# Half blocks and memory terms of an attention kernel: one product of 128 rows for both heads in place of two products of 64 rows

## The chip, the core and the metric

The kernel runs on one core of a Trainium2 chip. The metric is the time of one execution on the device in microseconds (us). Engines are named as in the profile: PE (TensorE, the matrix engine), PEld (its weight loads), DVE (VectorE), ACT (ScalarE), POOL (GpSimd), SP (SyncE, which issues the transfers here).

## The reference, cut to what matters

```python
# q, k, v: (B=2, H=8, S=576, D=64); M_prev (B,H,D,D); z_prev (B,H,D); beta (H)
a = softmax(causal(q @ k.T / 8));  local = a @ v
q_p = elu(q) + 1
mem_out = (q_p @ M_prev) / (q_p @ z_prev + 1e-6)
x = g * mem_out + (1 - g) * local                  # g = sigmoid(beta), per head
x = elu(x @ w_in) @ w_out                          # 1152 x 512, d_ff 2048
out = sum_e p[:, e] * (relu(x @ w1[e]) @ w2[e])    # 4 experts, 1024 wide
```

## The kernel before, in words

Two heads are worked on at once: head 0 of a pair lies on partitions 0 to 63, head 1 on 64 to 127. Twelve units do the attention. The four F units (`F0` to `F3`, one for each pair of heads) take the first 192 rows of both batches; eight R units (`R00`, `R10`, `R01`, ...: batch and pair) take the other 384 rows of a batch. Each unit makes scores (`score`, tiles `sF`, `sR`), exponentials (`ptF`, `ptR`), transposes them with an identity (`transposes`, tiles `tF`, `tR`), copies the transposes to SBUF (`evac`, tiles `pfF`, `pfR`) and multiplies them with values (`values`). `mem` multiplies the feature map of the queries (`ppF`, `ppR`) with the memory. Values and memory are held in one tile `rv` (`rvF`, `rvR`) of entries of 65 columns: 64 columns and one that gives the denominator. `sum_a`, `sum_i`, `sum_f`, `mem_a`, `mem_i`, `mem_f`, `both` and `turn` divide, add and transpose back into `x`.

A tile of 128 queries has full blocks of 128 keys for each head (`odd` 0 or 1 in the list `BLOCKS`), and one half block (`odd` 2): 64 keys of head 0 on partitions 0 to 63, 64 keys of head 1 on partitions 64 to 127. An R unit has three tiles with 4, 3 and 2 full blocks for each head: 18 full blocks and 3 half blocks, in groups of four (`trans`, `evac`, `values` of a group). The half block of a tile comes last, and takes two products of 64 rows (line 1384), one for each head. `mem` takes two products of 64 rows for each tile (line 1244). All results go to one tile `sums` of two PSUM banks, one for each head; a bank holds memory terms in its first half and values in its second.

The products of attention here are of plain float32: the profile shows each as two weight loads and two matmuls ("records"). The dense layers use a float32 in two rounded parts: three matmuls for one product (lines 278 to 280, `mm3`).

The order of the work is made by a planner (`Plan.order`) while the program is written: each step has an engine, an assumed cost, a rank and the steps that it needs, and the planner starts on each engine the step of lowest rank that can start. Where it thinks that PE would wait, in the first 140 us, it puts matmuls of zeros there (`keep_busy`, `nothing`, line 304). Dense work of the rows of the F units (`ua`, `da`, then `ub`, `db`) fills PE between the steps of the R units. Weights of the first dense layer come as 64-bit words: lines 225, 231 and 235 (ACT, DVE, DVE) make float32 of them, lines 245 and 249 (ACT, POOL) split them into `wh` and `wl`. When the last R unit is done, DVE, ACT and POOL make sums of its blocks (`xT1` to `xT4`, lines 702 to 718, and of weights `s`, line 601) for the second stage (`pa10A`, ...).

Of the kernel before, what the change touches and what calls it, by code (L numbers as in the profile page):

```python
# [8 lines left out]
F32 = mybir.dt.float32  # L9
# [7 lines left out]
B, H, S, D = 2, 8, 576, 64  # L17
# [3 lines left out]
P = 128  # L21
NPART = 4
DV = D + 1
# [7 lines left out]
TILES = {"F": [(64, 192), (64, 192), (0, 64)], "R": [(448, 576), (320, 448), (192, 320)]}  # L31
# [6 lines left out]
HALVES = {"F": 4, "R": 8}  # L38
MEMORY = {"F": 8, "R": 11}
ENTRIES = {"F": 10, "R": 12}  # L40

BLOCKS = {
    kind: [
        b for t, (_, ext) in enumerate(tiles)
        for b in [(t, odd, j) for odd in (0, 1) for j in range(ext // P)] + [(t, 2, ext // P)]
    ]
# [13 lines left out]
def tile_kernel(  # L60
# [12 lines left out]
    nc = tc.nc  # L73
# [97 lines left out]
    FEWEST = {"F": 1, "R": 0}  # L171
# [863 lines left out]

    def values_cost(blocks):

        return sum(0.224 if odd < 2 else 0.45 for _, odd, _ in blocks)

# [98 lines left out]
    def plan_unit(plan, kind, b, c, start, spare, slack):  # L1138
# [4 lines left out]
        width = sum(ext for _, ext in tiles)  # L1143
        widest, entries = 1344, ENTRIES["R"]
# [21 lines left out]
        def load_v():  # L1166
            unit["rv"] = atile([P, entries, DV], F32, tag="rv", name=f"rv{uid}")[:, :ENTRIES[kind]]
            nc.sync.dma_start(out=unit["rv"], in_=vm[kind][c] if kind == "F" else vm[kind][b, c])
# [64 lines left out]
        def side(what):  # L1233
            keep_busy(at["sums"][:, 0, 256 * what:256 * what + 256], 2 * FEWEST[kind])
            return at["sums"][:, :, 256 * what:256 * what + nt * DV].rearrange("p a (t d) -> p a t d", d=DV)

        def mem():
            unit["om"] = side(0)
# [129 lines left out]
        def values(g):  # L1368
            if g == 0:
                unit["ov"] = side(1)  # L1370
            for n, (t, odd, j) in enumerate(groups[g]):
                col, pf, nb = P * n, unit["p", g], tiles[t][1] // P
                if odd < 2:
                    at_ = t * 2 + odd if kind == "F" else odd * full + (nb - 1 - j if odd else j)
                    nc.tensor.matmul(  # L1375
                        unit["ov"][:, odd, t], pf[:, col:col + P], unit["rv"][:, at_], start=j == 0, stop=False
                    )
                    continue
                for bi, r0, r in parts_of(t):

                    at_ = HALVES[kind] + (t + bi if len(parts_of(t)) > 1 else t)
                    for o in (0, 1):
                        rows = slice(D * o, D * o + D)
                        nc.tensor.matmul(  # L1384
                            unit["ov"][r0:r0 + r, o, t], pf[rows, col + r0:col + r0 + r], unit["rv"][rows, at_],
                            start=nb == 0, stop=True,
                        )

        for g, blks in enumerate(groups):
# [12 lines left out]
            add(  # L1402
                f"values{g}", "pe", values_cost(blks), lambda g=g: values(g),
                [f"evac{g}", "load_v"] + [f"values{g - 1}"] * (g > 0), ["ov"] * (g == 0), ["ph"] + ["rv", "nm", "nm"] * final,
# [177 lines left out]
```

## Time and profile before

| what | value |
|---|---|
| time, median of 3 runs | 728.83 us (728.65 to 729.18) |
| the profiled execution: its own time | 729.03 us |
| its span in the trace | 727.2 us (1.83 us lie around it) |
| PE busy | 717.5 us, 99% of the span |
| POOL, DVE, ACT busy | 425.7, 396.7, 354.2 us |

The busy time of PE includes matmuls of zeros and matmuls at half clock, and matmuls overlap in the pipeline; so the starts of successive rows say more than the durations.

### The profile page before, as it was taken

The numbers are of one execution on the slowest core, as the hardware profiler recorded it, in microseconds if no ns is written. First come the engines' busy times: TensorE is split into PE (matmuls) and PEld (weight loads), VectorE is DVE, ScalarE is ACT, GpSimd is POOL, SyncE is SP. The second block draws the span as 40 slices with busy tenths as digits, with TensorE's granted clock in tenths as the row PEclk, the third lists the DMA queues.
The fourth block names the chain that finished last, engine by engine and source line by source line (L and its number), as shares of the span: only waits on it lengthen the run. The fifth ranks groups of instructions, "written<-read, shape, count | busy, mean of one in ns | idle before, by whom it ended". The sixth has DMA issues, their size and how long they took to land.

```text
span 727.2 us, 11034 instructions
## 1 busy us (share of the span) xinstructions
PE 717.5 (99%) x4255; PEld 643.9 (89%) x4255; DVE 396.7 (55%) x846; ACT 354.2 (49%) x610; POOL 425.7 (59%) x256
## 2 busy tenths in 40 slices
PE   9989999999999999998999999999999999999997
PEld 5768998888889888897999999998998989899896
DVE  4887785434353443435537474873635546364562
ACT  7768877454444543444568373753323324243130
POOL 5468688665536442259878763597656456664210
PEclk9999999999999999999999999999999999999999
DMA  7677985434233041221423021112312203021002
GB/s 260 214 267 266 388 294 165 143 106 136 87 108 109 31 138 32 85 91 55 159 88 116 30 87 59 59 33 84 116 40 77 88 29 117 30 88 58 1 1 87
DMA packets 23541, 80.36 MB, mean 110 GB/s; under 512 B 2881, under 2 KB 2881, under 8 KB 23489
## 3 DMA queue, kind: packets, MB, share of 16 engines
q1 hardware_dynamic: 23488, 79.66, 32.6%
q8 instruction: 33, 0.54, 0.3%
q14 instruction: 20, 0.16, 0.1%
HBM read 68.90 MB, written 10.75 MB: 110 GB/s over the span
## 4 chain that ended last, share of the span: by engine, by line
PE 96%; POOL 2%; DVE 1%; issue 0%; ACT 0%
PE db L278 9%; PE db L280 9%; PE db L279 9%; PE sums L1375 5%; PE da L278 5%; PE da L279 5%; PE da L280 5%; PE ub L278 3%; PE sR L1297 3%; PE ub L280 3%; PE ub L279 3%; PE tR L1359 3%; PE sums L1384 2%; PE ua L278 2%; PE ua L280 2%; PE ua L279 2%
## 5 line engine op out<-in xcount | busy, mean ns | idle before, releaser
L249 POOL TENSOR_TENSOR wl<-wr,wh 128x1024 fp32r<-128x1024 f32 x72 | 171.9, 2391 | 178.7 <-ACT wh L245 140.0
L245 ACT ACTIVATE wh<-wr 128x1024 fp32r<-128x1024 f32 x72 | 75.7, 1056 | 96.5 <-PE db L279 55.8
L278 PE MATMUL db<-wh,hb 128*128 128x512 f32 x288 | 115.6, 401 | 0.0
L280 PE MATMUL db<-wl,hb 128*128 128x512 f32 x288 | 113.4, 394 | 2.2 <-POOL wl L249 2.2
L279 PE MATMUL db<-wh,hb 128*128 128x512 f32 x288 | 113.0, 392 | 0.0
L997 DVE SCALAR_TENSOR_TENSOR acc<-db,pr,acc 128x512 f32<-128x512 f32 x42 | 31.5, 751 | 70.0 <-PE db L280 69.2
L280 PEld LDWEIGHTS db<-wl,hb 128*128 128x128 f32 x288 | 54.4, 189 | 14.3 <-POOL wl L249 2.6
L278 PE MATMUL da<-ha,wh 128*128 128x384 f32 x192 | 65.1, 339 | 0.0
L278 PEld LDWEIGHTS db<-wh,hb 128*128 128x128 f32 x288 | 54.5, 189 | 11.9 <-issue 1.4
L280 PE MATMUL da<-ha,wh 128*128 128x384 f32 x192 | 64.2, 334 | 0.0
L279 PE MATMUL da<-ha,wl 128*128 128x384 f32 x192 | 64.2, 334 | 0.0
L279 PEld LDWEIGHTS db<-wh,hb 128*128 128x128 f32 x288 | 54.5, 189 | 10.3
L278 PE MATMUL ub<-yh,wh 128*128 128x384 f32 x128 | 46.3, 362 | 0.0
L280 PE MATMUL ub<-yl,wh 128*128 128x384 f32 x128 | 43.1, 336 | 0.0
L279 PE MATMUL ub<-yh,wl 128*128 128x384 f32 x128 | 43.0, 336 | 0.0
L1375 PE MATMUL sums<-rvR,pfR 128*128 128x65 f32 x288 | 37.4, 271 | 0.0
L278 PEld LDWEIGHTS da<-ha,wh 128*128 128x128 f32 x192 | 36.1, 188 | 0.7 <-issue 0.4
L1375 PEld LDWEIGHTS sums<-rvR,pfR 128*128 128x128 f32 x288 | 35.3, 191 | 1.0
L279 PEld LDWEIGHTS da<-ha,wl 128*128 128x128 f32 x192 | 36.1, 188 | 0.0
L280 PEld LDWEIGHTS da<-ha,wh 128*128 128x128 f32 x192 | 36.0, 188 | 0.0
L537 DVE SCALAR_TENSOR_TENSOR acc<-db,pr,acc 128x512 f32<-128x512 f32 x21 | 15.7, 749 | 36.4 <-PE db L280 36.3
L1320 ACT ACTIVATE ptR<-ptR,nmR 128x576 f32<-128x576 f32 (+2 forms) x48 | 29.9, 659 | 10.2 <-DVE nmR L1311 10.2
(860 smaller groups left out, 1838.1 us busy)
## 6 DMA issues: line engine op xcount, KB each, us to landing
wr<-in_w SPq DMA_DIRECT2D x64, 512.0 KB, 3.5
w<-in_w SPq DMA_DIRECT2D x32, 512.0 KB, 5.8
wscr<-wr SPq DMA_DIRECT2D x16, 512.0 KB, 6.9
wr<-wscr SPq DMA_DIRECT2D x16, 512.0 KB, 3.3
qkR<-in_qk_r SPq DMA_DIRECT2D x8, 480.0 KB, 5.0
rvR<-in_vm_r SPq DMA_DIRECT2D x8, 390.0 KB, 4.0
out<-acc SPq DMA_DIRECT2D x8, 256.0 KB, 2.0
qkF<-in_qk_f SPq DMA_DIRECT2D x4, 416.0 KB, 3.8
```

The lines of the kernel that those rows point to most:

```text
L245: nc.scalar.activation(out=t["wh"], in_=t["wr"], func=AF.Copy)
L249: nc.gpsimd.tensor_tensor(out=wl, in0=t["wr"], in1=f32(t["wh"]), op=ALU.subtract)
L278: nc.tensor.matmul(out, ah, bh, start=first, stop=False)
L279: nc.tensor.matmul(out, al, bh, start=False, stop=False)
L280: nc.tensor.matmul(out, ah, bl, start=False, stop=last)
L537: nc.vector.scalar_tensor_tensor(out=acc, in0=t["ps"], scalar=p, in1=acc, op0=ALU.mult, op1=ALU.add)
L997: nc.vector.scalar_tensor_tensor(out=acc, in0=t["ps"], scalar=p, in1=acc, op0=ALU.mult, op1=ALU.add)
L1297: nc.tensor.matmul(unit["s", odd, t, n][:, :w], unit[x][rows, q], unit[y][rows, ks[odd]], start=m == 0 and r0 == 0, stop=m == 2 and final,)
L1320: nc.scalar.activation(out=blk, in_=blk, func=AF.Exp, scale=-1.0, bias=unit["nm"][odd][:, k:k + 1])
L1359: nc.tensor.transpose(pst[:, P * n:P * n + P], src, ident)
L1375: nc.tensor.matmul(unit["ov"][:, odd, t], pf[:, col:col + P], unit["rv"][:, at_], start=j == 0, stop=False)
L1384: nc.tensor.matmul(unit["ov"][r0:r0 + r, o, t], pf[rows, col + r0:col + r0 + r], unit["rv"][rows, at_], start=nb == 0, stop=True,)
```

## The change

It puts the half block of a tile first in its list, gives memory terms and values a bank each (`om`, `ov`) with the two heads side by side, and takes both heads in one product of 128 rows and 130 columns: the moving operand has head 0's numbers in columns 0 to 64 of rows 0 to 63, head 1's in columns 65 to 129 of rows 64 to 127, and zeros elsewhere. The zeros are written on the host, so `rv` grows from 10 (F) and 12 (R) entries to 16. The planner is told of one cost for all products, and `mem` of an F unit no longer waits for the `sum_f` of the F unit before it. The full blocks' products stay as they are, but now add to what the half block has begun.

```diff
-MEMORY = {"F": 8, "R": 11}
-ENTRIES = {"F": 10, "R": 12}
+MEMORY = {"F": 12, "R": 14}
+ENTRIES = 16
...
-        for b in [(t, odd, j) for odd in (0, 1) for j in range(ext // P)] + [(t, 2, ext // P)]
+        for b in [(t, 2, ext // P)] + [(t, odd, j) for odd in (0, 1) for j in range(ext // P)]
...
-        at["sums"] = at["o"].tile([P, 2, 512], F32, tag="o", name="sums")
+        at["om"], at["ov"] = (at["o"].tile([P, 512], F32, tag=x, name=x) for x in ("om", "ov"))
...
-        return sum(0.224 if odd < 2 else 0.45 for _, odd, _ in blocks)
+        return 0.06 + 0.224 * sum(2 if kind == "F" and (t, odd) == (2, 2) else 1 for t, odd, _ in blocks)
...
-            keep_busy(at["sums"][:, 0, 256 * what:256 * what + 256], 2 * FEWEST[kind])
-            return at["sums"][:, :, 256 * what:256 * what + nt * DV].rearrange("p a (t d) -> p a t d", d=DV)
+            keep_busy(at[what], FEWEST[kind])
+            unit[what] = at[what][:, :nt * 2 * DV].rearrange("p (t a d) -> p a t d", a=2, d=DV)
+
+        def pair(what, t, r0, r):
+            return at[what][r0:r0 + r, 2 * DV * t:2 * DV * t + 2 * DV]
+
+        def apart(entry):
+            return unit["rv"][:, entry:entry + 2].rearrange("p a d -> p (a d)")
...
-                    for odd in (0, 1):
-                        rows = slice(D * odd, D * odd + D)
-                        nc.tensor.matmul(
-                            unit["om"][r0:r0 + r, odd, t], unit["phi"][rows, q:q + r],
-                            unit["rv"][rows, MEMORY[kind] + bi], start=True, stop=True,
-                        )
+                    nc.tensor.matmul(
+                        pair("om", t, r0, r), unit["phi"][:, q:q + r], apart(MEMORY[kind] + 2 * bi), start=True, stop=True,
+                    )
...
-        mem_cost = 0.2 + 0.224 * sum(len(parts_of(t)) for t in range(nt))
-        before = [(f"F{c - 1}", "sum_f")] if kind == "F" and c else []
-        add("mem", "pe", mem_cost, mem, ["phi", "load_v", *before], ["om"], ["pp"])
+        mem_cost = 0.06 + 0.224 * sum(len(parts_of(t)) for t in range(nt))
+        add("mem", "pe", mem_cost, mem, ["phi", "load_v"], ["om"], ["pp"])
...
-                        unit["ov"][:, odd, t], pf[:, col:col + P], unit["rv"][:, at_], start=j == 0, stop=False
+                        unit["ov"][:, odd, t], pf[:, col:col + P], unit["rv"][:, at_], start=False, stop=odd == 1 and j == nb - 1
...
-                    for o in (0, 1):
-                        rows = slice(D * o, D * o + D)
-                        nc.tensor.matmul(
-                            unit["ov"][r0:r0 + r, o, t], pf[rows, col + r0:col + r0 + r], unit["rv"][rows, at_],
-                            start=nb == 0, stop=True,
-                        )
+                    nc.tensor.matmul(
+                        pair("ov", t, r0, r), pf[:, col + r0:col + r0 + r], apart(at_), start=True, stop=nb == 0,
+                    )
```

Because the planner works with other costs, the order of the steps changes too. Three places follow.

On PE, the third and fourth group of the second R unit before: transposes (line 1359), the half block's two products of 64 rows (line 1384) and full blocks (line 1375).

```order
L1359 MATMUL tR_1697<-ident,ptR_1387 128x128 x4
L1384 MATMUL sums<-rvR_1289,pfR_1689 128x65 x2
L1375 MATMUL sums<-rvR_1289,pfR_1689 128x65 x3
L1359 MATMUL tR_1716<-ident,ptR_1387 128x128 x4
L1375 MATMUL sums<-rvR_1289,pfR_1711 128x65 x3
L1384 MATMUL sums<-rvR_1289,pfR_1711 128x65 x2
```

The same unit's third group in the changed program, where the half block is line 1384 with 130 columns and the full blocks line 1377, up to the dense matmul after it.

```order
L1361 MATMUL tR_1987<-ident,ptR_1807 128x128 x4
L1377 MATMUL ov<-rvR_1466,pfR_1980 128x65
L1384 MATMUL ov<-rvR_1466,pfR_1980 128x130
L1377 MATMUL ov<-rvR_1466,pfR_1980 128x65 x2
L278 MATMUL db_2007<-wh_1671,hb_1785 128x512
```

Two products have become one, and it stands between full blocks. Over the whole program, 48 products of `mem` and 48 of half blocks in R units become 24 and 24, and 32 and 32 in F units become 16 and 16.

On DVE, from the end of `F2` to the end of `F3` before: the steps of line 1223, 1264 and 1229 on `nm_F` are `mem` of `F3`, line 1364 is the copy of its last transposes, lines 231 and 235 are weight words.

```order
L1223 SCALAR_TENSOR_TENSOR nm_F_633<-sums,wmem 128x6
L1264 RECIPROCAL nm_F_633<-nm_F_633 128x6
L1229 TENSOR_TENSOR sums<-sums,nm_F_633 128x2x3x64
L231 TENSOR_SCALAR wr_550<-wr_550 128x512
L1364 COPY pfF_654<-tF_644 128x384
L1430 TENSOR_TENSOR xl_101<-xF_639,xh_100 128x384
L235 SCALAR_TENSOR_TENSOR wr_550<-w_2_0_371,wr_550 128x512
L231 TENSOR_SCALAR wr_550<-wr_550 128x512
L1223 SCALAR_TENSOR_TENSOR nv_F_673<-sums,wloc 128x6
```

The same stretch of the changed program (the copy is line 1366).

```order
L1223 SCALAR_TENSOR_TENSOR nm_F_580<-om,wmem 128x6
L1266 RECIPROCAL nm_F_580<-nm_F_580 128x6
L1229 TENSOR_TENSOR om<-om,nm_F_580 128x2x3x64
L231 TENSOR_SCALAR wr_434<-wr_434 128x512
L235 SCALAR_TENSOR_TENSOR wr_434<-w_1_0_258,wr_434 128x512
L1429 TENSOR_TENSOR xl_101<-xF_587,xh_100 128x384
L1366 COPY pfF_612<-tF_604 128x384
L231 TENSOR_SCALAR wr_434<-wr_434 128x512
L235 SCALAR_TENSOR_TENSOR wr_434<-w_1_1_309,wr_434 128x512
L1223 SCALAR_TENSOR_TENSOR nv_F_627<-ov,wloc 128x6
```

The weight words that stand here are those of the second weight tile (`w_1`), where before they were those of the third (`w_2`): by the end of `F3` DVE has done four steps of line 231 and four of line 235, before it had done six and five.

On POOL, from the last R unit's sum (line 1416) to the last weight of the first stage before: `xT1l` to `xT4l` (line 705) and `s` (line 601) are for the second stage, `wl` (line 249) is the last weight tile that the first stage's `db` needs.

```order
L1416 TENSOR_TENSOR tvR_3529<-tvR_3529,tmR_3371 128x384
L249 TENSOR_TENSOR wl_3576<-wr_3526,wh_3569 128x1024
L705 TENSOR_TENSOR xT1l<-xT_3609,xT1h 128x384 x2
L705 TENSOR_TENSOR xT2l<-xT_3626,xT2h 128x384
L601 TENSOR_TENSOR s_48_0_3787<-wr_3783 128x512
L705 TENSOR_TENSOR xT2l<-xT_3626,xT2h 128x384
L705 TENSOR_TENSOR xT3l<-xT_3634,xT3h 128x384 x2
L601 TENSOR_TENSOR s_48_0_3787<-s_48_0_3787,wr_3781 128x512
L705 TENSOR_TENSOR xT4l<-xT_3656,xT4h 128x384
L601 TENSOR_TENSOR s_48_2_3793<-wr_3781,wr_3783 128x512
L705 TENSOR_TENSOR xT4l<-xT_3656,xT4h 128x384
L249 TENSOR_TENSOR wl_3697<-wr_3551,wh_3666 128x1024
```

The same in the changed program.

```order
L1415 TENSOR_TENSOR tvR_3435<-tvR_3435,tmR_3299 128x384
L249 TENSOR_TENSOR wl_3512<-wr_3457,wh_3498 128x1024
L601 TENSOR_TENSOR s_48_0_3715<-wr_3708 128x512
L705 TENSOR_TENSOR xT1l<-xT_3548,xT1h 128x384 x2
L705 TENSOR_TENSOR xT2l<-xT_3555,xT2h 128x384 x2
L705 TENSOR_TENSOR xT3l<-xT_3573,xT3h 128x384 x2
L705 TENSOR_TENSOR xT4l<-xT_3582,xT4h 128x384 x2
L249 TENSOR_TENSOR wl_3639<-wr_3480,wh_3598 128x1024
L622 TENSOR_TENSOR wl48A_3713<-wr_3706,wh48A_3712 128x1024
L601 TENSOR_TENSOR s_48_0_3715<-s_48_0_3715,wr_3706 128x512
```

Of the three steps `s` between `xT1l` and `wl`, one now stands ahead of them and two behind. On PE, between the last unit's `turn` (`xR`) and the second stage stood 36 `db`, 36 `ub` and 36 `db`; now it is 27 `db`, 36 `ub` and 36 `db`. The matmuls of zeros change as well: at the first R unit 4 on `sR` and 2 on `ua` become 7 on `sR` and 10 on `da` (128x384), and the `turn` of `F3` has 6 ahead of it where it had 7.

## Rows read from the trace of the kernel before

**Rows 1.** The page: the span, and part 1 for PE, PEld, DVE, ACT, POOL.

```profile
span 727.2 us, 11034 instructions
...
PE 717.5 (99%) x4255; PEld 643.9 (89%) x4255; DVE 396.7 (55%) x846; ACT 354.2 (49%) x610; POOL 425.7 (59%) x256
```

**Rows 2.** The page: the chain that ended last, by engine.

```profile
PE 96%; POOL 2%; DVE 1%; issue 0%; ACT 0%
```

**Rows 3.** Windows: length, busy PE, PEld, DVE, ACT, POOL; granted clock, DMA share, GB/s.

```profile
40.00:48.00 8.00, 8.00 (x47) 5.70 (x47) 6.72 (x14) 3.60 (x5) 2.27 (x1) 0.79 0.55 183
...
80.00:100.00 20.00, 20.00 (x128) 19.11 (x127) 15.94 (x32) 16.38 (x29) 19.33 (x13) 1.00 0.92 334
...
345.00:350.00 5.00, 5.00 (x18) 3.96 (x18) 0.75 (x1) 2.12 (x2) 5.00 (x4) 0.76 0.21 79
```

**Rows 4.** Timeline of PE (start, length): `mem` of R00 between dense matmuls.

```profile
61.47 0.34 PE L280 MATMUL da<-ha,wh 128*128 128x384 f32 x1
61.74 0.89 PE L1244 MATMUL sums<-rvR,ppR 64*128 64x65 f32 x12
...
62.84 0.34 PE L279 MATMUL da<-ha,wl 128*128 128x384 f32 x1
```

**Rows 5.** Timeline of PE: a group of four full blocks of R00.

```profile
66.33 0.60 PE L1359 MATMUL tR<-ident,ptR 128*128 128x128 f32 x4
66.77 1.00 PE L1375 MATMUL sums<-rvR,pfR 128*128 128x65 f32 x8
67.58 0.42 PE L278 MATMUL da<-ha,wh 128*128 128x384 f32 x1
67.84 0.33 PE L279 MATMUL da<-ha,wl 128*128 128x384 f32 x1
```

**Rows 6.** Timeline of PE, narrow window: second to fourth record of that group.

```profile
66.83 0.50 PE L1375 MATMUL sums<-rvR,pfR 128*128 128x65 f32 x3
```

**Rows 7.** Timeline of PE: a group with the half block first.

```profile
71.89 0.60 PE L1359 MATMUL tR<-ident,ptR 128*128 128x128 f32 x4
72.42 0.44 PE L1384 MATMUL sums<-rvR,pfR 64*128 64x65 f32 x4
...
73.74 0.34 PE L279 MATMUL da<-ha,wl 128*128 128x384 f32 x1
```

**Rows 8.** Timeline of PE: a group with the half block last.

```profile
75.66 0.60 PE L1359 MATMUL tR<-ident,ptR 128*128 128x128 f32 x4
...
77.46 0.34 PE L279 MATMUL ua<-xh,wl 128*128 128x384 f32 x1
```

**Rows 9.** Timeline of PE: a half block alone between dense matmuls.

```profile
80.22 0.34 PE L280 MATMUL ua<-xl,wh 128*128 128x384 f32 x1
...
81.14 0.34 PE L279 MATMUL ua<-xh,wl 128*128 128x384 f32 x1
```

**Rows 10.** Timeline, end of F3: idle time and its releaser in brackets.

```profile
37.31 1.74 DVE L231 TENSOR_SCALAR wr<-wr 128x512 int32<-128x512 int32 x1
...
39.58 0.44 PE L1375 MATMUL sums<-rvF,pfF 128*128 128x65 f32 x2 [2.32 <-DVE pfF L1364]
...
40.76 3.08 PE L304 MATMUL xF<-zeros 128*128 128x512 bf16 x7
```

**Rows 11.** Timeline, end of the first stage: POOL and PE.

```profile
338.04 1.30 POOL L601 TENSOR_TENSOR s<-wr,wr 128x512 f32<-128x512 f32 x1
...
338.44 0.39 PE L278 MATMUL db<-wh,hb 128*128 128x512 f32 x1
...
340.06 0.40 PE L279 MATMUL db<-wh,hb 128*128 128x512 f32 x1
342.67 0.50 PE L280 MATMUL db<-wl,hb 128*128 128x512 f32 x1 [2.21 <-POOL wl L249]
...
350.78 0.33 PE L278 MATMUL pa10A<-xB11h,wh48A 128*128 128x384 f32 x1
```

**Rows 12.** Timeline of SP: the load of R00's values.

```profile
32.97 0.38 SPq L1168 DMA_DIRECT2D rvR<-in_vm_r  x1
```

More of the change, by code (lines that the diff above doesn't have):

```diff
@@ L1034, in pool_cost, with values_cost @@
         return 2.1e-3 * n + 0.2
-    def values_cost(blocks):
-        return sum(0.224 if odd < 2 else 0.45 for _, odd, _ in blocks)
+    def values_cost(kind, blocks):
+        return 0.06 + 0.224 * sum(2 if kind == "F" and (t, odd) == (2, 2) else 1 for t, odd, _ in blocks)
     class Plan:
@@ L1143, in plan_unit @@
         width = sum(ext for _, ext in tiles)
-        widest, entries = 1344, ENTRIES["R"]
+        widest = 1344
         unit, uid = {}, f"F{c}" if kind == "F" else f"R{b}{c}"
@@ L1166, in load_v @@
         def load_v():
-            unit["rv"] = atile([P, entries, DV], F32, tag="rv", name=f"rv{uid}")[:, :ENTRIES[kind]]
+            unit["rv"] = atile([P, ENTRIES, DV], F32, tag="rv", name=f"rv{uid}")
             nc.sync.dma_start(out=unit["rv"], in_=vm[kind][c] if kind == "F" else vm[kind][b, c])
@@ L1233, in side @@
         def side(what):
-            keep_busy(at["sums"][:, 0, 256 * what:256 * what + 256], 2 * FEWEST[kind])
-            return at["sums"][:, :, 256 * what:256 * what + nt * DV].rearrange("p a (t d) -> p a t d", d=DV)
+            keep_busy(at[what], FEWEST[kind])
[4 more added lines that the diff above has]
+            return unit["rv"][:, entry:entry + 2].rearrange("p a d -> p (a d)")
         def mem():
-            unit["om"] = side(0)
+            side("om")
             for t in range(nt):
@@ L1369, in values @@
             if g == 0:
-                unit["ov"] = side(1)
+                side("ov")
             for n, (t, odd, j) in enumerate(groups[g]):
@@ L1379, in values @@
                 for bi, r0, r in parts_of(t):
-                    at_ = HALVES[kind] + (t + bi if len(parts_of(t)) > 1 else t)
-                    for o in (0, 1):
-                        rows = slice(D * o, D * o + D)
-                        nc.tensor.matmul(
-                            unit["ov"][r0:r0 + r, o, t], pf[rows, col + r0:col + r0 + r], unit["rv"][rows, at_],
-                            start=nb == 0, stop=True,
-                        )
+                    at_ = HALVES[kind] + 2 * (t + bi if len(parts_of(t)) > 1 else t)
+                    nc.tensor.matmul(
+                        pair("ov", t, r0, r), pf[:, col + r0:col + r0 + r], apart(at_), start=True, stop=nb == 0,
+                    )
         for g, blks in enumerate(groups):
@@ L1402, in plan_unit @@
             add(
-                f"values{g}", "pe", values_cost(blks), lambda g=g: values(g),
+                f"values{g}", "pe", values_cost(kind, blks), lambda g=g: values(g),
                 [f"evac{g}", "load_v"] + [f"values{g - 1}"] * (g > 0), ["ov"] * (g == 0), ["ph"] + ["rv", "nm", "nm"] * final,
@@ L1516, in halves, with apart @@
         return np.concatenate([vones[b, :, odd, first:first + D][:, turn[odd]] for odd in (0, 1)], 1)
+    def apart(x):
+        parts = np.zeros((2, *x.shape), np.float32)
+        for odd in (0, 1):
+            rows = slice(D * odd, D * odd + D)
+            parts[odd, :, rows] = x[:, rows]
+        return list(parts)
     def heads(x):
@@ L1530 @@
     vm_f = [block(b, odd, 0) for b in (0, 1) for odd in (0, 1)]
-    vm_f += [halves(b, first) for first in (P, 0) for b in (0, 1)] + [mz[0], mz[1]]
+    for x in [halves(b, first) for first in (P, 0) for b in (0, 1)] + [mz[0], mz[1]]:
+        vm_f += apart(x)
     vm_f = np.stack(vm_f, 2)
@@ L1535 @@
         vs = [block(b, odd, P * j) for odd in (0, 1) for j in range(4)]
-        vm_r.append(np.stack(vs + [halves(b, q0 + D) for q0, _ in TILES["R"]] + [mz[b]], 2))
+        for x in [halves(b, q0 + D) for q0, _ in TILES["R"]] + [mz[b]]:
+            vs += apart(x)
+        vm_r.append(np.stack(vs, 2))
     vm_r = np.stack(vm_r)
```

## The prediction

> **What bounds the kernel now.** First the page's busy times: PE 717.5 of 727.2 us, the next engine, POOL, 425.7 [rows 1]. Then the chain that ended last, 96% of it PE [rows 2]: what PE does in order is what the time is made of, and time saved there comes back unless PE then waits. Third the windows, to see where PE is busy without getting on: at 40 to 48 us the granted clock is 0.79 and at 345 to 350 us 0.76, where a busy stretch has 1.00 [rows 3]. Last the timeline at those places and inside one R unit. The slow stretches follow two waits: 2.32 us on DVE's copy of transposes at the end of F3, after a step of line 231 of 1.74 us ahead of it [rows 10], and 2.21 us on POOL's `wl` at the end of the first stage [rows 11]. So there are three things to cost: PE's work in the R units, the F phase, and the end of the first stage.
>
> **PE's work in an R unit.** I take starts, not durations. Inside a group of full blocks the eight records of four products run from 66.77 to the next start at 67.58 [rows 5]; the second starts 0.06 us after the first, the others follow at (67.58 - 66.83) / 7 = 0.11 us [rows 5, 6]. So a product in a stream costs 0.22 us. The whole group of four, from the first transpose to the second dense matmul behind it, takes 67.84 - 66.33 = 1.51 us [rows 5].
> - A group with the half block first takes 73.74 - 71.89 = 1.85 us [rows 7]. New, it is a group of four products in which one has 130 columns: 1.51. Saved: 0.34.
> - With the half block last, 77.46 - 75.66 = 1.80 us [rows 8]. Saved: 0.29.
> - A half block alone takes 81.14 - 80.22 = 0.92 us, of which two dense matmuls at 0.17 would take 0.35 anyway: 0.57 [rows 9]. In its place stands one product: 0.22 and what it costs to go in and out. Out is 0.09 (67.84 - 67.58 is 0.26 in place of 0.17 [rows 5]); in is not shown for this pair, between 0 and 0.10, I take 0.06. So 0.37. Saved: 0.20.
> - `mem` takes 62.84 - 61.47 = 1.37 us, less 0.35 gives 1.02 [rows 4]. New: three products, 0.66, and 0.15 in and out. Saved: 0.21.
>
> That is 1.04 us for a unit if a record of 130 columns keeps the pace of 0.11. Before has no such record. The bounds come from the 65 columns: their stream takes at most the 0.06 us between the first two records [rows 5, 6], so 130 take some 0.12, which the weight pass of 0.11 nearly hides; only where the weights are already there (behind transposes, where 65 columns showed 0.06) is 0.05 added, some three times a unit. At the other end, if the short first spacing says nothing of the stream, 65 columns could fill the whole 0.11 and 130 would take 0.22. I take the first, since a spacing of 0.06 with a later record right behind it leaves no room for a stream of 0.11. So 1.04 - 0.15 = 0.89 for a unit, **7.1 us** for eight. The ends: 8.3 us saved without the addition; and with 0.11 more on each of the 96 new records (48 products of two), 10.6 us lost, that is 3.5 us slower.
>
> The rows also show where the saving comes from. The twelve records of 64 rows of `mem` start within 61.74 to 62.55 at the latest, so two heads' records share a slot of 0.11; what costs is the change between 64 and 128 rows, 61.47 to 61.74 = 0.27 where a dense matmul follows at 0.17 [rows 4]. The Trainium skill (TensorEngine Tiling (Array Packing), Key Properties and When to Use Tiling) says that with a contraction of 64 two row tiles work in parallel, up to twice as fast, and that changing the tiling mode drains the engine. Its first rule speaks against this change, since the pairs use exactly that; its second speaks for it. By the first alone the R units would give nothing; by the rows, 7.1 us. The trace agrees with both: pairs at one slot, and a step of 0.10 at the change.
>
> The full blocks keep their products. The larger `rv` costs transfers only: R00's values are issued at 32.97 us and first used at 61.74 [rows 4, 12], so a third more bytes are hidden by some 28 us of other work; if that lead were gone they would cost about half a microsecond a unit at the 334 GB/s of a busy stretch [rows 3].
>
> **The F phase.** A product for both heads saves PE little here, but the order changes. On DVE `mem` of F3 now comes with no wait for F2's end, and three steps of weight words (two of line 231, one of 235) go behind F3's end; the copy that PE waited 2.32 us for has one step of 231 and one of 235 ahead of it, beside which PE has other products. If the wait goes, the clock should hold, and the zeros ahead of F3's `turn` (now 6, before 7 in 3.08 us, 0.44 each at the low clock [rows 10]) take half of that each: 1.3 us. I put the end of F3 **3.0 us** earlier: 1.7 from the zeros, 1.3 of the 2.32. The bounds are 0 and 4.0. What is late next is the weights: their words are three steps behind. The planner fills this with zeros: 17 against 6 at the first R unit, 3 more of 512 columns (0.22) and 8 more of 384 (0.17 each, as a dense matmul of that width [rows 4]), **2.0 us** lost. Net 1.0 us saved, between 2.0 saved and 3 lost, the loss if the weights' words make PE wait as well: at 80 to 100 us POOL is busy 19.33 of 20 us and the transfers' share is 0.92 [rows 3], so there is little to catch up with.
>
> **The end of the first stage.** PE goes at 0.23 a `db` (338.44 to 340.06 is seven steps), stops at 340.06, and reaches `pa10A` at 350.78: 10.72 us for 28 steps that need 6.5 [rows 11]. So the stop and the half clock behind it cost 4.2 us. In the new order PE has 9 `db` fewer between the last `turn` and this place, so it comes 2.1 us sooner; but POOL has three steps `s` of 1.3 us fewer (338.04 is one [rows 11]) between `xT1l` and `wl`, so the weight comes 3.9 us sooner, if `s` ahead of `xT1l` fits into POOL's wait for it. The wait of 2.4 to 2.6 us would shrink to 0.7, too short, I think, for the clock to fall. Saved: 3.5; I take **3.0**, between 4.2 saved and 1.5 lost (the one `s` in front of `xT1l` holds it up by its 1.3).
>
> **Sum.** 7.1 + 1.0 + 3.0 = 11.1 us from the profiled execution's 729.03: 717.9. That execution lies 0.2 above the median of 728.83, so the median after is put at **717.7 us**.
>
> **Rivals.**
> - *The stall at the end of the first stage stays* (or goes to the next step of POOL, `swl48S`, behind which two `s` now stand). For it: POOL has no idle time at 345 to 350 us [rows 3]. Against: the three `s` are gone from that stretch. 717.7 + 3.0 = 720.7.
> - *The weights are late in the first 100 us.* PE comes to them 3 us sooner, they three steps of DVE later. For it: the transfers' 0.92 and POOL's 19.33 of 20 [rows 3]. Against: before, PE had no wait at all in 80 to 100 us. The F phase then loses 3 instead of saving 1: 721.7, and 724.7 together with the first rival.
> - *The pairs cost no more than the new product.* Two heads' records share a slot of 0.11 [rows 4]; if going in and out costs the new product as much as the pair, the R units give nothing: 717.7 + 7.1 = 724.8. The rule on row tiles above would have it so. Against: the difference of 0.29 to 0.34 between groups that differ in one half block [rows 5, 7, 8].
> - *Slower: 130 columns set the pace of a record,* at 0.22 us in place of 0.11. The R units then lose 3.5 us, and the F units, whose 32 new products of two records get 64 times 0.11 = 7 us longer where they saved nothing before, lose the 3 us at their end and 4 more. 3.5 + 4 + 2.0 - 3.0 = 6.5: about 735.5. All terms together turn at a pace of about 0.18 us. Against: the spacing of 0.06 us [rows 6].
>
> **Chances.** The forecast 0.48; the first stall stays 0.22; weights late, with or without it, 0.13; more than forecast (both ends of the R units and the F phase, about 713) 0.05; no gain in the R units 0.05, a third of which loses the other gains too; slower 0.07. The range for 8 in 10 goes from 711.5 to 724.5: it leaves out the slower case and the worst of the others. Faster by over 0.2% (1.5 us, about what a measurement of this kernel can tell from no change): 0.90; within 0.2%: 0.03; slower: 0.07.
>
> **What would show it.** Right: groups of four with a half block at 1.5 to 1.6 us, records of 130 columns at 0.11 to 0.12; `mem` alone at 1.15; no wait on DVE's copy at the end of F3 and full clock in 32 to 48 us; a wait for `wl` under 1 us before `pa10A`. Wrong: records of 130 columns 0.2 apart; waits of PE on `wl` or `wh` between 45 and 100 us; a low clock again around 340 us. From the end of the first stage on, the order is the same and PE is busy, so the time after `pa10A` should be the same to a few tenths.

## The result, and the profile after

The changed kernel takes 719.0 us (median of 4 runs, 718.8 to 719.41) where the kernel before takes 728.74 beside it: ratio 0.9873, interval 0.9861 to 0.9885. The profiled execution takes 718.8 us. The page of the changed kernel, the span, PE's part of the busy times, and the chain that ended last by engine (before: [rows 1, 2]):

```profile
span 717.0 us, 10716 instructions
...
PE 706.3 (99%) x4099; PEld 640.0 (89%) x4099; DVE 392.6 (55%) x846; ACT 354.3 (49%) x610; POOL 426.0 (59%) x256
...
PE 88%; POOL 3%; DVE 3%; DMA 2%; ACT 2%; issue 1%; SPq 0%; DVEq 0%; ACTq 0%
```

PE is still 99% busy, but its share of the chain fell from 96 to 88: at a few places the end is now set by waits on other engines. Windows of the changed kernel, columns as in [rows 3]:

```profile
40.00:48.00 8.00, 7.98 (x46) 7.53 (x45) 6.49 (x10) 4.71 (x8) 4.29 (x3) 1.00 0.64 197
48.00:56.00 8.00, 6.40 (x37) 4.72 (x37) 6.33 (x14) 7.55 (x16) 8.00 (x7) 1.00 0.95 309
...
345.00:350.00 5.00, 4.55 (x27) 4.23 (x26) 4.27 (x9) 4.63 (x8) 5.00 (x3) 1.00 0.45 144
```

Both stretches of low clock are gone: 0.79 and 0.76, means over windows in which the clock stood at 1.2 GHz for a part and at 2.4 GHz for the rest, became 1.00, all of it at 2.4 GHz. PE has new idle time at 48 to 56 and at 345 to 350 us. To see where the 10.2 us of span went, I take the starts of four rows of PE in the timeline: the first `ua`, the last R unit's `turn` (`xR`), and the first rows of the second stage (`pa10A`) and of its second part (`pb10A`). The third column is an experiment told below.

| start, us | before | changed | new products, old order |
|---|---|---|---|
| first `ua` (end of the F units) | 44.69 | 40.27 | 42.20 |
| last `turn` of an R unit | 323.66 | 316.51 | 312.32 |
| `pa10A` | 350.78 | 339.75 | 337.83 |
| `pb10A` | 475.60 | 465.38 | 462.66 |

The changed kernel has nine more `db` ahead of the last `turn` (2.1 us at 0.23 each), so 316.51 stands for 314.4 there. Its F units gain 4.4 us; the stretch of the R units gains 4.8, which leaves 8.4 for PE's products once 3.6 for more zeros (2.0) and a wait on a weight word (1.6) are set against them; the end of the first stage gains 1.8, and 0.8 is lost behind it. Timeline of PE in the changed kernel: the end of F3 (as [rows 10]) and the first R unit's zeros, a group of four with the half block (as [rows 5, 7]), and `mem` alone (as [rows 4], between `db`):

```profile
36.43 0.66 PE L1377 MATMUL ov<-rvF,pfF 128*128 128x65 f32 x4 [0.65 <-DVE pfF L1366]
37.39 1.47 PE L304 MATMUL xF<-zeros 128*128 128x512 bf16 x6
...
50.81 1.67 PE L304 MATMUL sR<-zeros 128*128 128x512 bf16 x7 [1.60 <-DVE wr L235]
...
66.79 0.60 PE L1361 MATMUL tR<-ident,ptR 128*128 128x128 f32 x4
67.22 0.39 PE L1384 MATMUL ov<-rvR,pfR 128*128 128x130 f32 x2
67.45 0.78 PE L1377 MATMUL ov<-rvR,pfR 128*128 128x65 f32 x6
68.03 0.42 PE L278 MATMUL da<-ha,wh 128*128 128x384 f32 x1
68.29 0.33 PE L279 MATMUL da<-ha,wl 128*128 128x384 f32 x1
...
178.77 0.39 PE L280 MATMUL db<-wl,hb 128*128 128x512 f32 x1
179.00 0.83 PE L1248 MATMUL om<-rvR,ppR 128*128 128x130 f32 x6
...
179.90 0.39 PE L279 MATMUL db<-wh,hb 128*128 128x512 f32 x1
```

The group takes 68.29 - 66.79 = 1.50 us, as much as four full blocks did; `mem` takes 1.13. The wait on DVE's copy is 0.65 where it was 2.32, the zeros behind it run at full speed (0.24 each), and a wait of 1.60 us on a weight word stands ahead of the first R unit. Of the ten zeros on `da` only five are there; the other five, which the section on the change puts at the first R unit too, come at 101.37 us. The end of the first stage, POOL and PE:

```profile
319.89 1.62 POOL L601 TENSOR_TENSOR s<-wr 128x512 f32<-128x512 f32 x1 [3.42 <-DMA wr<-wscr]
321.48 2.62 POOL L705 TENSOR_TENSOR xT1l<-xT,xT1h 128x384 fp32r<-128x384 f32 x2
...
330.87 2.34 POOL L249 TENSOR_TENSOR wl<-wr,wh 128x1024 fp32r<-128x1024 f32 x1
...
333.27 0.50 PE L280 MATMUL db<-wl,hb 128*128 128x512 f32 x1 [1.97 <-POOL wl L249]
...
339.75 0.33 PE L278 MATMUL pa10A<-xB11h,wh48A 128*128 128x384 f32 x1
...
345.84 0.45 PE L279 MATMUL pa10S<-xT3h,swl48S 128*128 128x384 f32 x1 [0.45 <-POOL swl48S L622]
```

The wait for `wl` is nearly as long as before (1.97 for 2.21), but the matmuls behind it keep their pace of 0.23: from the wait's end to `pa10A` 6.48 us, where it was 350.78 - 342.67 = 8.11 [rows 11].

### The profile page after: what moved, and what is told of

It is laid out like the page before. It is cut to its first block, busy times and chain, and to the rows that moved or that the text cites. A ratio compares the mean times of both kernels' runs of the same rounds, so it can differ in the third digit from the quotient of the medians.

```text
span 717.0 us, 10716 instructions
## 1 busy us (share of the span) xinstructions
PE 706.3 (99%) x4099; PEld 640.0 (89%) x4099; DVE 392.6 (55%) x846; ACT 354.3 (49%) x610; POOL 426.0 (59%) x256
## 4 chain that ended last, share of the span: by engine, by line
PE 88%; POOL 3%; DVE 3%; DMA 2%; ACT 2%; issue 1%; SPq 0%; DVEq 0%; ACTq 0%
PE db L278 9%; PE db L280 8%; PE db L279 8%; PE ov L1377 4%; PE da L278 4%; PE da L279 4%; PE da L280 4%; PE ub L278 3%; PE sR L1299 3%; PE tR L1361 3%; PE ub L280 3%; PE ub L279 3%; PE ov L1384 1%; PE om L1248 1%; PE ua L278 1%; PE ua L280 1%
## 5 line engine op out<-in xcount | busy, mean ns | idle before, releaser
L997 DVE SCALAR_TENSOR_TENSOR acc<-db,pr,acc 128x512 f32<-128x512 f32 x42 | 31.5, 751 | 69.9 <-PE db L280 69.2
L1377 PE MATMUL ov<-rvR,pfR 128*128 128x65 f32 x288 | 38.3, 265 | 0.0
L1377 PEld LDWEIGHTS ov<-rvR,pfR 128*128 128x128 f32 x288 | 37.2, 191 | 0.2
L1322 ACT ACTIVATE ptR<-ptR,nmR 128x576 f32<-128x576 f32 (+2 forms) x48 | 29.8, 659 | 10.3 <-DVE nmR L1313 10.2
L506 ACT ACTIVATE hb<-ub 128x384 fp32r<-128x384 f32 x32 | 15.7, 491 | 38.2 <-PE ub L280 38.2
```

What stands on the lines that cost most here:

```text
L506: nc.scalar.activation(out=t["h"][:, 0], in_=t["ps"], func=AF.Relu)
L997: nc.vector.scalar_tensor_tensor(out=acc, in0=t["ps"], scalar=p, in1=acc, op0=ALU.mult, op1=ALU.add)
L1322: nc.scalar.activation(out=blk, in_=blk, func=AF.Exp, scale=-1.0, bias=unit["nm"][odd][:, k:k + 1])
L1377: nc.tensor.matmul(unit["ov"][:, odd, t], pf[:, col:col + P], unit["rv"][:, at_], start=False, stop=odd == 1 and j == nb - 1)
```

## The experiments

Ratios are to the kernel before, run beside each (medians 728.1 to 728.5 us). The changed kernel itself (719.0 us, its runs 0.6 us apart) was not run beside them, so I read nothing into a difference to it of less than 0.7 us.

**The products without their order** (`new_products_old_order`): the half block last again (with the `start` and `stop` of the products to match), the planner's old costs and the old wait of `mem` in the F units.

```diff
-        for b in [(t, 2, ext // P)] + [(t, odd, j) for odd in (0, 1) for j in range(ext // P)]
+        for b in [(t, odd, j) for odd in (0, 1) for j in range(ext // P)] + [(t, 2, ext // P)]
...
-        return 0.06 + 0.224 * sum(2 if kind == "F" and (t, odd) == (2, 2) else 1 for t, odd, _ in blocks)
+        return sum(0.224 if odd < 2 else 0.45 for _, odd, _ in blocks)
...
-        mem_cost = 0.06 + 0.224 * sum(len(parts_of(t)) for t in range(nt))
-        add("mem", "pe", mem_cost, mem, ["phi", "load_v"], ["om"], ["pp"])
+        mem_cost = 0.2 + 0.224 * sum(len(parts_of(t)) for t in range(nt))
+        before = [(f"F{c - 1}", "sum_f")] if kind == "F" and c else []
+        add("mem", "pe", mem_cost, mem, ["phi", "load_v", *before], ["om"], ["pp"])
...
```

> The products of 128 rows and 130 columns and the banks om and ov stay, but every step on every engine stands where it stood before the change: the half block is last in its tile again, the planner has its old costs, and mem of an F unit waits for the sums of the F unit before it. Theory (the products give the R units' 7 us, the order gives the rest): the R units lose the 7 us, the stall at the end of F3 (2.3 us) and the half clock behind the stall at the end of the first stage stay, so about 721.5 us; mem alone at 1.13 us, groups with a half block at 1.5 to 1.6 us. Rival (the new order gave the gain, the pairs cost as little as the new product): 727 to 729 us, as before.

Measured 716.94 us (716.07 to 718.16), ratio 0.9847 (0.9831 to 0.9862): faster than both forecasts and 2 us faster than the changed kernel. The rival falls. The theory's time is missed by 4.6 us: the products give more than its 7, and the two waits that were to stay cost less, as told below. The profiled execution is the fastest of the four (716.07). Its timeline can be held against [rows 4, 7 to 9] place by place, since the order is the same:

```profile
58.99 0.34 PE L280 MATMUL da<-ha,wh 128*128 128x384 f32 x1
59.16 0.83 PE L1248 MATMUL om<-rvR,ppR 128*128 128x130 f32 x6
...
60.01 0.34 PE L279 MATMUL da<-ha,wl 128*128 128x384 f32 x1
...
69.02 0.60 PE L1362 MATMUL tR<-ident,ptR 128*128 128x128 f32 x4
...
70.52 0.33 PE L279 MATMUL da<-ha,wl 128*128 128x384 f32 x1
...
72.46 0.60 PE L1362 MATMUL tR<-ident,ptR 128*128 128x128 f32 x4
...
73.96 0.33 PE L279 MATMUL ua<-xh,wl 128*128 128x384 f32 x1
...
76.73 0.34 PE L280 MATMUL ua<-xl,wh 128*128 128x384 f32 x1
76.90 0.38 PE L1385 MATMUL ov<-rvR,pfR 128*128 128x130 f32 x2
...
77.30 0.34 PE L279 MATMUL ua<-xh,wl 128*128 128x384 f32 x1
```

`mem` alone takes 1.02 us (before 1.37), the group with the half block first 1.50 (1.85), last 1.50 (1.80), the half block alone 0.57 (0.92). From the first `ua` to the last `turn` the same work takes 312.32 - 42.20 = 270.1 us in place of 279.0: 8.9 us for eight units, 1.11 each. Not every place gives the same. Where `mem` stands between products of 128 rows (four of the eight units) it gives 0.30 to 0.36 us; where it stands beside `score`, whose products have 64 rows themselves, it gives nothing (three units; from 97.88 to 99.70 before, 1.82 us, from 94.06 to 95.87 here, 1.81) or loses 0.11 (the last unit, between `score` and a `turn`). So it is the change of rows that is saved. All `mem` together give 1.25 us, all half blocks 7.5. The stall at the end of F3, which both theories left in place, shrank without any change of order, from a wait of 2.32 us with seven zeros at the low clock behind it to waits of 0.65 and 1.37 with the clock at 1.00; the first `ua` comes 2.5 us sooner. The wait for `wl` at the end of the first stage is as long as before (2.17), but the clock holds behind it as well: 312.32 to 337.83 is 25.5 us, where it was 27.1. DVE and PE at the end of F3:

```profile
35.92 0.42 DVE L231 TENSOR_SCALAR wr<-wr 128x512 int32<-128x512 int32 x1
36.45 0.56 DVE L1367 COPY pfF<-tF 128x384 f32<-128x384 f32 x1
...
37.06 0.44 PE L1378 MATMUL ov<-rvF,pfF 128*128 128x65 f32 x2 [0.65 <-DVE pfF L1367]
...
37.39 1.81 DVE L235 SCALAR_TENSOR_TENSOR wr<-w,wr 128x512 int32<-128x512 int32 x1
...
41.14 0.55 PE L1422 MATMUL xF<-ident,tvF 128*128 128x128 f32 x3 [1.37 <-DVE tvF L1416]
```

The step of line 231 took 1.74 us before [rows 10] and 0.42 here. In the kernel before, it started while POOL had a `wl` under way, and so late because the step ahead of it waited:

```profile
36.41 0.17 DVE L1223 SCALAR_TENSOR_TENSOR nm_F<-sums,wmem 128x6 f32<-128x6 f32 x1 [1.17 <-PE sums L1375]
...
36.41 2.36 POOL L249 TENSOR_TENSOR wl<-wr,wh 128x1024 fp32r<-128x1024 f32 x1 [2.18 <-ACT wh L245]
```

By the trace, DVE's reading of the memory terms waited for the last values that PE wrote to the same tile of two banks. With a bank each for memory terms and values that wait is gone (no run has the banks without the products), DVE reaches line 231 at 35.92, just ahead of POOL's `wl` at 36.29, and now the next such step, line 235 at 37.39, is the long one. That a long step waits for POOL is tested below.

**One product for each head** (`one_head_each`).

```diff
-                    nc.tensor.matmul(
-                        pair("ov", t, r0, r), pf[:, col + r0:col + r0 + r], apart(at_), start=True, stop=nb == 0,
-                    )
+                    for o in (0, 1):
+                        nc.tensor.matmul(
+                            pair("ov", t, r0, r)[:, DV * o:DV * o + DV], pf[:, col + r0:col + r0 + r],
+                            unit["rv"][:, at_ + o], start=o == 0, stop=nb == 0 and o == 1,
+                        )
```

(`mem` in the same way.)

> The changed kernel in its order, but each product of 130 columns is made as two products of 128 rows and 65 columns, one for each head (with the other head's zeros): there is no change between 64 and 128 rows any more, but two places of 0.22 us for one. Theory (the gain is one slot saved in each place, and the steps at the change of rows are the smaller part): 48 more products in the R units at 0.22 us give 10.7 us, those of the F units up to as much per product where PE does not wait there, so 729 to 733 us. Rival (the gain is only that rows no longer change, and a second product of the same rows is cheap, under 0.06 us): 719 to 722 us.

Measured 732.51 us (732.23 to 733.18), ratio 1.0061 (1.0046 to 1.0076): slower than the kernel before. The theory holds. `mem` alone between `db`:

```profile
186.72 0.39 PE L280 MATMUL db<-wl,hb 128*128 128x512 f32 x1
186.95 1.45 PE L1249 MATMUL om<-rvR,ppR 128*128 128x65 f32 x12
...
188.52 0.40 PE L279 MATMUL db<-wh,hb 128*128 128x512 f32 x1
```

1.80 us, where the changed kernel has 1.13: three products more, 0.22 each. So the old pairs of 64 rows (0.35 dearer than the new product in [rows 4]) were cheaper than two products of 128 rows (0.67 dearer): the pairs did share slots, and lost part of it at the change of rows. The Trainium skill (TensorEngine Tiling (Array Packing), Key Properties and When to Use Tiling) has both rules, the parallel row tiles and the drain at a change of mode; the runs agree with both.

**Wider products** (`mem_260_columns`): the memory's entries stand twice in the moving operand of `mem` in two tiles of an R unit, and the second half of the result is overwritten.

```diff
+                    if kind == "R" and t < 2:
+                        nc.tensor.matmul(
+                            at["om"][:, 2 * DV * t:2 * DV * t + 4 * DV].rearrange("p (n e) -> p n e", n=2),
+                            unit["phi"][:, q:q + r],
+                            apart(MEMORY[kind]).unsqueeze(1).to_broadcast([P, 2, 2 * DV]), start=True, stop=True,
+                        )
+                        continue
```

> The changed kernel, but mem of an R unit takes 260 columns in place of 130 for its first two tiles (the memory's entries twice; the second half is overwritten by the next tile's product): 16 products, 32 records. Theory (a record's pace is set by its weights at 0.11 us, and columns cost nothing until they take longer than that; estimated from 65 columns in the 0.06 us between the first two records, 130 columns take just over 0.11 and 260 some 0.22): 32 times 0.11 = 3.4 us more, 722.2 us, records of 260 columns 0.22 us apart. Rival (the stream is hidden well past 130 columns): 719 us, records at 0.11. Rival (columns set the pace already at 130 and the first product's weights hide the rest): records 0.2 apart with no sharp step, over 723 us.

Measured 722.82 us (722.55 to 723.25), ratio 0.9928 (0.9912 to 0.9945), 3.8 us over the changed kernel. The theory holds:

```profile
62.97 1.04 PE L1249 MATMUL om<-rvR,ppR 128*128 128x260 f32 x4
63.85 0.39 PE L1255 MATMUL om<-rvR,ppR 128*128 128x130 f32 x2
```

Four records of 260 columns take 63.85 - 62.97 = 0.88 us, 0.22 each, twice the pace of 65 and of 130 columns. If the pace goes with the columns there, 130 would take some 0.11 by themselves (an estimate; no run has a width between 130 and 260): the new product stands near the width at which a wider operand begins to cost.

**Without the zeros at the first R unit** (`no_zeros_at_R00`).

```diff
-    IDLE_END = 140.0
+    IDLE_END = 40.0
```

> The changed kernel without the 17 matmuls of zeros that the planner puts ahead of the first R unit's values (7 of 512 columns and 10 of 384); all else in the same order. If they fill no wait, their whole time comes back: 7 times 0.22 and 10 times 0.17 are 3.2 us, 715.8 us. If the weights' words are what PE would wait for there (the changed kernel waits 1.6 us for one of them between the zeros), the time comes back only in part or not at all: 718 to 719.5 us. If the wait that opens lowers the granted clock: 719.5 to 722 us.

Measured 721.44 us (720.16 to 722.28), ratio 0.9906 (0.9891 to 0.9921): 2.4 us slower than the changed kernel, by the third expectation. Of the 17 zeros, twelve stood at the first R unit and five at 101.37 us. The page of waits puts 3.4 us on line 235, and the clock behind them is low, which it never was with the zeros:

```profile
52.00:56.00 4.00, 2.66 (x13) 2.28 (x14) 3.20 (x9) 4.00 (x9) 4.00 (x4) 0.87 0.90 363
56.00:60.00 4.00, 4.00 (x19) 3.75 (x20) 2.34 (x4) 2.19 (x4) 4.00 (x4) 0.71 0.98 336
```

About 1 us of the difference lies elsewhere (a wait of 1.04 us on ACT at 11.33, which the changed kernel does not have). From the last `ua` ahead of the place to the first `da` it takes 4.34 us here (49.90 to 54.24) and 5.01 with the zeros (48.87 to 53.88), so the zeros cost 0.7 us; without them eleven matmuls behind the wait go at the low clock (54.88 to 58.35 is 3.5 us, most at 0.32 each in place of 0.17) and lose 1.6. Most of the zeros' time the weights would have taken anyway: the words were late, as rival two had it.

**The last weight's low part on DVE**, in the changed kernel (`after_wl_on_dve`), in the kernel before (`before_wl_on_dve`) and with the old order (`old_order_wl_on_dve`).

```diff
-            nc.gpsimd.tensor_tensor(out=wl, in0=t["wr"], in1=f32(t["wh"]), op=ALU.subtract)
+            eng = nc.vector if i == NW1 + NW2 - 1 else nc.gpsimd
+            eng.tensor_tensor(out=wl, in0=t["wr"], in1=f32(t["wh"]), op=ALU.subtract)
...
```

(The planner is told of the engine in the same way.)

> The changed kernel, but the low part (wl) of the last weight of the first stage is made on DVE in place of POOL; PE's order is the same. Theory (the wait of 2.4 us ahead of pa10A is on POOL's row of steps s, xT, wl, with one s in front of xT1l): the wait goes, and the step behind it, swl48S, which PE waited 0.8 us for, comes sooner as well: 2.4 to 3.2 us less, about 716 us. Rival (another step, xT4l or DVE's own sums, is as late as wl, and the wait only changes its name): 718.5 to 719.5 us.

> The kernel before with the same move of the last wl from POOL to DVE; PE's order is the same as before. It prices the stall at the end of the first stage where the clock fell behind it. Theory (the wait of 2.2 us is POOL's and the low clock of the 10 us behind it comes from the wait): wait and half clock go together, 4.2 us less, 724.6 us, granted clock 1.00 at 340 to 350 us. Rival (the clock falls there for another reason than this wait): 2.2 us less, 726.6 us, granted clock still under 0.9. Rival (another step is as late): 728 to 729 us.

> The new products in the old order, with the last wl of the first stage on DVE in place of POOL. PE's order is that of the new products in the old order. If the two add up (the products and the order are one thing, the stall at the end of the first stage another): its wait of 2.2 us goes as in the changed kernel, where the same move gave 2.1 us: 714.8 us. If another step (DVE's hb, xT) is as late: 716 to 717 us.

Measured 716.94 us (716.56 to 717.48), ratio 0.9847 (0.9833 to 0.986); 725.82 us (725.18 to 726.28), ratio 0.9968 (0.9955 to 0.998); and 714.58 us (714.27 to 716.49), ratio 0.9814 (0.9796 to 0.9832). In the changed kernel the move gives 2.1 us, somewhat under the forecast, and with the old order 2.4: the stall at the end of the first stage is POOL's row of steps, and adds to the rest. A step of DVE (`hb`) is late next: PE waits 0.71 us for it at 329.87.

In the kernel before, the median falls by 2.6 us, between the theory (4.2) and its first rival (2.2). In the profiled execution `pa10A` comes 3.2 us sooner (347.57) than in the profile of before, where the low clock was there to lose, with short waits for `hb` (on ACT's step, then on DVE's, 0.8 us in all) taking most of the rest of the 4.2. The clock at 345 to 350 us is 1.00, as the theory has it:

```profile
345.00:350.00 5.00, 5.00 (x27) 4.53 (x26) 1.57 (x3) 1.55 (x2) 5.00 (x4) 1.00 0.45 152
```

**Shorter instructions on POOL**, in the kernel before (`before_wl_split`), the changed one (`after_wl_split`), and the old order with the last `wl` on DVE as well (`old_order_both`).

```diff
-            nc.gpsimd.tensor_tensor(out=wl, in0=t["wr"], in1=f32(t["wh"]), op=ALU.subtract)
+            for c in range(0, 1024, 256 if i < 2 else 1024):
+                cs = slice(c, c + (256 if i < 2 else 1024))
+                nc.gpsimd.tensor_tensor(out=wl[:, cs], in0=t["wr"][:, cs], in1=f32(t["wh"][:, cs]), op=ALU.subtract)
```

> The kernel before with wl of the first two weights in four instructions of 256 columns on POOL in place of one of 1024; all orders as before. Theory (DVE's step of line 231 at the end of F3, 1.74 us where it takes 0.42 alone, stands still until the instruction that POOL has under way is done, as every long one of lines 231 and 235 ends just behind a wl): it now waits for a quarter of wl, 0.6 us, or for what is left of it, so 231 takes about 1 us, the copy behind it comes 0.7 to 1.3 us sooner, PE's wait of 2.3 us shrinks by as much, and if the clock holds then, the zeros behind it give 1.5 us more: 726 to 728 us. Rival (DVE is slow there for another reason, or waits for all four): 231 stays at 1.7 us, 728 to 729 us.

> The changed kernel with wl of the first two weights in four instructions of 256 columns on POOL; all orders as in the changed kernel. There the step of line 231 at 39.07 takes 2.18 us, and PE waits 1.6 us at 48.9 for a step of line 235 that stands some steps behind it on DVE. Theory (DVE's step waits for POOL's instruction): 231 takes about 1 us, the words come about 1.1 us sooner, the wait of 1.6 us shrinks to 0.5: 717.9 us. Rival (the words are late for their transfers or for ACT, not for this step): the wait stays, 719 us. Rival (not POOL's instruction): 231 stays over 2 us, 719 us.

> The new products in the old order, the last wl of the first stage on DVE, and wl of the first two weights in four instructions. Against the kernel with the first two alone: the step of line 235 of 1.81 us ahead of the end of F3 gets shorter by about 1.1 us, and PE's wait of 1.4 us on tvF with it: 713.7 us. If zeros or another wait take its place: 714.8 us.

Measured 726.62 us (725.65 to 728.69), ratio 0.9978 (0.9967 to 0.9988); 719.06 us (718.23 to 719.55), ratio 0.9869 (0.9852 to 0.9885); 714.04 us (714.01 to 714.63), ratio 0.9803 (0.9787 to 0.9819). In the kernel before the theory holds: the step of line 231 ends after 0.84 us, the wait behind it is 1.42 in place of 2.32.

```profile
36.07 2.96 POOL L251 TENSOR_TENSOR wl<-wr,wh 128x256 fp32r<-128x256 f32 x4 [2.18 <-ACT wh L245]
...
36.94 0.84 DVE L231 TENSOR_SCALAR wr<-wr 128x512 int32<-128x512 int32 x1
...
38.29 0.44 PE L1377 MATMUL sums<-rvF,pfF 128*128 128x65 f32 x2 [1.42 <-DVE pfF L1366]
39.31 2.84 PE L306 MATMUL xF<-zeros 128*128 128x512 bf16 x7
```

The seven zeros behind it still run low (0.41 each): the clock fell behind this shorter wait too. In the changed kernel line 231 fell from 2.18 to 0.54 us, but the wait of 1.60 on the word only to 1.2, and the time not at all: the mechanism holds, my theory that this step made the word late does not. With the old order the split gives 0.5 us, within what I can tell. This last kernel, at 714.04 us, is the fastest of the study, 5 us under the changed one.

**Half of the order** (`old_f_order`: old costs and the old wait of `mem` for the F units alone; `old_r_order`: old costs for the R units alone).

```diff
+        if kind == "F":
+            return sum(0.224 if odd < 2 else 0.45 for _, odd, _ in blocks)
+        return 0.06 + 0.224 * len(blocks)
...
```

> The changed kernel, but the planner has its old costs and the old wait of mem for the F units; those of the R units are the new ones. The planner then puts 9 zeros of 384 columns at the first R unit in place of 17 (7 of 512, 10 of 384) and 5 ahead of them. Theory (the 2 us by which the changed kernel is slower than the new products in the old order lie in the F phase: it ends 1.9 us sooner, but zeros of 2.0 us, and a wait of 1.6 us on late weights' words, take more): the wait on line 235 at 49 us goes, the first ub comes at about 134.5 us in place of 135.9, the end of the first stage stays as in the changed kernel: 717.6 us. Rival (the 2 us lie in the R units' order, at the end of the first stage): 719 us.

> The changed kernel, but the planner has its old costs for the R units; those of the F units, and mem without the wait, are the new ones. Theory (F phase): the first ub at about 135.9 us as in the changed kernel, with the wait on line 235; only the wait of 0.8 us on swl48S behind pa10A can go: 718.2 to 719 us. Rival (the 2 us lie in the R units' order): 717 us.

Measured 720.13 us (719.34 to 720.6), ratio 0.9877 (0.9854 to 0.99), and 723.68 us (721.89 to 725.94), ratio 0.9924 (0.99 to 0.9948). Both theories fail: neither half of the old order gives the 2 us. In the first kernel another step of DVE starts behind POOL's `wl`, and the stall of F3 is longer than it ever was:

```profile
36.74 2.36 POOL L249 TENSOR_TENSOR wl<-wr,wh 128x1024 fp32r<-128x1024 f32 x1 [2.19 <-ACT wh L245]
36.83 2.82 DVE L235 SCALAR_TENSOR_TENSOR wr<-w,wr 128x512 int32<-128x512 int32 x1
...
40.17 0.66 PE L1380 MATMUL ov<-rvF,pfF 128*128 128x65 f32 x4 [3.31 <-DVE pfF L1369]
```

Its first `ua` comes at 45.34, later than before and 5.1 us later than in the changed kernel; yet its last `turn` comes at 316.83, only 0.3 us later. It has no wait on line 235 at the first R unit and two zeros in place of twelve there: what the changed kernel gains at the end of F3 is for the most part taken again by zeros and late words. In the second, PE waits twice for words of line 235 (1.6 us each) and once for DVE's `yl` (1.1). The order of such a plan does not split into parts whose prices add: a step moved by half a microsecond decides whether it meets `wl`.

## Why the prediction was right, and where its terms were off

The profiled time was put at 717.9 and was 718.8. Of what was to show it, the groups (1.50 us), the records of 130 columns (67.22 to 67.45 is two, 0.11 each) and `mem` (1.13) came as told; a wait of 0.65 us on DVE's copy was left, the one on `wl` did not go under 1 us, and the time behind `pa10A` grew by 0.8. Four terms were off, two each way; that they cancelled to 0.9 us is luck.

- **R units: 7.1 forecast, 8.4 found** (8.9 in the old order). The mechanism is the one named: with the order held, each of the four places of R00 gives 0.30 to 0.35 us, and the mean unit 1.11 in all. The lone half block gives 0.35 (I had 0.20): going in and out of a product with all rows costs less than I took from [rows 5]. `mem` gives 0.35 in R00 (I had 0.21) but only 0.16 in the mean unit, since beside `score` it gives nothing, which I had not looked at. The deduction of 0.15 a unit for 130 columns does not show. Both rivals about the products fall: pairs among products of 128 rows are not as cheap as the new product, and 130 columns do not set a pace of 0.22; but 260 do.
- **F phase: 3.0 sooner forecast, 4.4 found.** 2.5 come with the products and their banks alone, which I had priced at little. The prediction gave the end of the wait to the moved steps of DVE; with no step moved the wait shrinks as well, by the trace because of the bank of their own and because line 231 then starts ahead of POOL's `wl`.
- **First R unit: 2.0 lost forecast, 3.6 found.** The number of zeros is right, though five of the 17 stand at 101.37 us and not at the first R unit; the 1.6 is a wait on a late word, rival two in small. Without the zeros it is 3.4, so PE reached the words too early by more than the zeros hide.
- **End of the first stage: 3.0 forecast, 1.0 found**, rival one in its main part. The failed step is that the `s` ahead of `xT1l` would fit into POOL's wait. Against the old order with the new products, `xT1l` to `wl` is 3.9 us shorter, as forecast (330.87 - 321.48 = 9.4, there 328.92 - 315.62 = 13.3), and PE comes 2.0 us sooner after `turn`; but `xT1l` starts 4.97 us after `turn` in place of 3.30. So 2.2 us on POOL stand against 2.0 on PE, and the wait stays. That the clock held behind it saved 1.6 all the same, and the wait on `swl48S` behind the two moved `s` took most of the 0.8 that is lost behind `pa10A` (345.05 to 346.12 is 1.07 us for two steps of 0.17).

Sum of the misses: 1.3 and 1.4 us better, 1.6 and 2.0 worse, 0.9 over in all. The order itself, which the prediction counted as a gain of 4, is worth 2 us less than the old one under the same products (719.0 against 716.94, medians).

What stays open: why the weights' words are late in the changed order after the split of `wl`, and what decides whether the clock falls behind a wait. At the end of the first stage it fell behind 2.21 us in the profile of before and held behind 2.19 in the kernel with `wl` split, where PE's order is the same; at the end of F3 it fell behind 1.42 there and held behind 1.37 with the new products in the old order. Each of these is one execution, and the same program does not always do the same: the runs of the kernel before have a mean granted clock of 0.994 to 0.996 in most (727.3 to 729.3 us), 0.998 in some (727.3 to 727.8) and 0.989 to 0.992 in a few (731.1 to 731.8). So the 1.6 us that the clock saves at the end of the first stage is the price in the profiled execution, not in each.

## What to carry to other kernels

Where two half-height products stand among full ones, cost the change of rows at both ends and not only the slots: a zero-padded product for both was 0.3 us cheaper in each such place and no cheaper beside other products of 64 rows, with columns that kept a record's pace (130 at 0.11 us; 260 took 0.22). Cost the products and the order that they cause apart, by running one with the other's order: here the order took back 2 us. Of a wait that one engine's row of steps sets, check what each moved step waits for itself, since one `s` that waited for its transfer held up all that stood behind it.

## What I had not expected of the hardware

A step of DVE on weight words in SBUF stands still while POOL's subtraction of two SBUF tiles is under way: line 231 takes 0.42 us alone, 1.74 and 2.18 beside `wl` of 2.36, and 0.84 and 0.54 when `wl` comes in quarters; line 235 takes 0.69 and up to 2.82. Each long one ends just behind an instruction of POOL. The Trainium skill says so (SBUF — State Buffer, Who interferes with whom): DVE and GpSimd share a pair of ports, which the one that starts first keeps for its whole instruction. The runs agree. For the later weights the words' first form lies in `cv`, a tile in PSUM, and not in `wr`; there the same line runs beside `wl` at its own pace of 0.69. Both cases in the changed kernel:

```profile
38.60 2.36 POOL L249 TENSOR_TENSOR wl<-wr,wh 128x1024 fp32r<-128x1024 f32 x1 [5.72 <-ACT wh L245]
39.07 2.18 DVE L231 TENSOR_SCALAR wr<-wr 128x512 int32<-128x512 int32 x1
...
44.68 2.42 POOL L249 TENSOR_TENSOR wl<-wr,wh 128x1024 fp32r<-128x1024 f32 x1 [3.71 <-ACT wh L245]
44.75 0.69 DVE L231 TENSOR_SCALAR cv<-cv 128x512 int32<-128x512 int32 x1
```
